# Attention and a gated feed-forward layer on one core: a weight's sign made on GpSimd, the byte of its low word written into it, and all engine orders worked out anew

## The chip, the cores and the metric

The kernel runs on one core of a Trainium2 chip. The metric is the device time of one execution in microseconds (us), as a median of several runs. The engines are called PE (TensorE, the matmuls), DVE (VectorE), ACT (ScalarE), POOL (GpSimd) and SP (SyncE, which here only issues transfers). Each engine works through its own instructions in the order in which they stand; engines wait for each other by semaphores.

## The reference

```python
def attention(q, k, v):                      # 8 batches, 8 heads, 576 positions, 64 wide
    k_p = k.reshape(B, H, 72, 8, D).mean(axis=3)
    v_p = v.reshape(B, H, 72, 8, D).mean(axis=3)
    scores = scale * np.matmul(q, k_p.transpose(0, 1, 3, 2))
    attn = np.exp(scores - np.max(scores, axis=-1, keepdims=True))
    attn = attn / (np.sum(attn, axis=-1, keepdims=True) + 1e-09)
    return np.matmul(attn, v_p)

x = attention(q, k, v)                       # as 4608 tokens x 512
h = x @ w_in                                 # 512 -> 2048
g = h * np.clip(h + 3.0, 0.0, 6.0) / 6.0
out = g @ w_out                              # 2048 -> 512
```

`w_in` and `w_out` come as 64-bit floats, seen as pairs of 32-bit words; everything else is 32-bit.

## The kernel before

The 4608 tokens are worked off in blocks of 512, 256 and then 384 tokens. While the feed-forward products of one block run, the attention of the blocks behind it is worked in between them. The first four blocks (`Block`, products at L965 and L995) take each 32-bit operand as a sum of two parts, `hi` and `lo`, and so need the weights as such pairs. The last eight blocks go in four pairs (`super_block`, products `psx` at L1245 and L1368) by seven products of sums of halves; their operands are split likewise (`part`, L1226 on ACT and L1227 on DVE), and their weights come back from a scratch copy in device memory (tiles `wsFalse` and `wsTrue`, loaded by SP).

The weights are made ready once, in 16 slices `f` of the 2048-wide dimension, in class `Prep`. Slices 0 and 15 go in two parts of 128x512 (a half of `w_in`, a half of `w_out`), the other fourteen in one part of 128x1024 each: 18 parts. Each part's raw words lie in `raw`, and a float of 32 bits is put together in a buffer `u` by six steps:

- `low` (L873, ACT) turns the top byte of the low word into a small integer, written to `u` as a 32-bit integer;
- `sign` (L878, DVE) ors the sign bit of the high word into `u`;
- `scale` (L884, ACT) multiplies the high word, taken as a float, by 2^-111, in place;
- `join` (L889, DVE) ors the scaled high word, shifted left by 3, into `u`;
- `hi` (L913, ACT) rounds `u` to the matmul's format into the weight tile `w`;
- `lo` (L918, DVE) subtracts `hi` from `u`.

There are two buffers `u` for slices 0 to 14, one for the even and one for the odd ones.

At the start, ahead of all this, PE runs 26 matmuls on a unit matrix that nobody reads (`idle`, L461), then the first scores (L596) from `kbd` (L410, pooled keys) and the queries. From a product the chain of a tile of attention goes through DVE (`mx`, L600), ACT (the exponentials, L604), DVE (`sm`, L617 to L621), POOL or DVE (the division, L632 and L638), PE (a transposition, L691 and L693), DVE and ACT (its copies `a` and `arem`, L694 and L695), PE again (L772) and ACT and DVE (`xhi`, `xlo`, L777 and L778) to the operand of the feed-forward products.

Later batches take their keys from tiles `kst` (L388, a transfer on SP), which DVE pools (`ksum`, L402) and ACT places (`kbd`, L410), and their values from tiles `vst` (L421 and L424), which DVE adds up in place (L518) and splits (`vhi` L529 on ACT, `vlo` L530 on DVE). `kst`, `vst` and some others share a ring of four buffers: a load waits until the last reader of the tile that had the buffer is through, and what stands behind it on SP waits too.

The order of each engine's instructions isn't that of the code: `put_in_order` takes a table of numbers for each engine (`ORDER`: PE, DVE, Activation, Pool, SP), which says which instruction of those that the code records stands next.

Of the kernel before, what the change touches and what calls it, by code (L numbers as in the profile page):

```python
# [8 lines left out]
F32 = mybir.dt.float32  # L9
# [249 lines left out]
def attention_moe_kernel(  # L259
# [584 lines left out]
    class Prep:  # L844
# [695 lines left out]
    def run(steps, lag, attention, first_slot=0, preps={}, more=(), hooks={}, share=1.0):  # L1540
# [5 lines left out]
        for u in range(len(steps) + lag):  # L1546
            slot = paced.slot if u >= first_slot else no_slot
            if u < len(steps):
# [4 lines left out]
                if k == NF - 1:  # L1553
                    prep(k, "scale", "low", part=0)
# [115 lines left out]
```

## Time and profile before

| | |
|---|---|
| time, median of 3 runs | 882.92 us (880.13 to 883.78) |
| the profiled execution | 882.52 us, of which the span of its core is 880.6 us |
| mean granted TensorE clock | 0.998 of full speed |
| PE busy | 866.7 us, 98% of the span |
| DVE busy | 677.3 us, 77% |
| ACT busy | 555.9 us, 63% |
| POOL busy | 86.2 us, 10% |

The span runs from the first to the last instruction of the core; the 1.9 us between it and the time of the execution lie around it. A busy share is an average over stages that have different limits.

### The profile page before, as it was taken

How to read it: one execution, taken by the hardware profiler on the slowest of the kernel's cores; microseconds unless marked ns; L12 is line 12 of the kernel's file. 1: busy time of each engine (PE TensorE's matmuls, PEld its weight loads, DVE VectorE, ACT ScalarE, POOL GpSimd, SP SyncE). 2: the span in 40 equal slices, each digit the busy share in tenths (PEclk: the TensorE clock that was granted, in tenths of full speed). 3: DMA queues.
4: the chain of work that ended last, by engine and by line, in shares of the span. 5: the costliest groups of instructions: out<-in, count | busy, mean ns of one | idle time of the engine just before them, and what ended most of it. 6: DMA issues, size and time to landing. Idle time of an engine off the chain costs nothing.

```text
span 880.6 us, 15638 instructions
## 1 busy us (share of the span) xinstructions
PE 866.7 (98%) x5360; PEld 814.2 (92%) x5360; DVE 677.3 (77%) x1340; ACT 555.9 (63%) x1515; POOL 86.2 (10%) x168
## 2 busy tenths in 40 slices
PE   8899999999999999999999999999999999999998
PEld 7788888999999999999888999989999999999998
DVE  5999964677786677887989788897788888466764
ACT  5998666665667564777444777656687756355442
POOL 4100001110211110101000201100111100000000
PEclk9999999999999999999999999999999999999999
DMA  9934314223357998986779978976987777877884
GB/s 323 364 124 157 100 33 138 73 58 111 105 176 254 298 285 265 361 289 194 241 231 289 307 269 286 306 261 203 319 269 242 218 242 245 284 252 242 274 263 135
DMA packets 124654, 200.00 MB, mean 227 GB/s; under 512 B 13216, under 2 KB 81056, under 8 KB 124576
## 3 DMA queue, kind: packets, MB, share of 16 engines
q1 hardware_dynamic: 124432, 199.00, 69.1%
q8 instruction: 43, 0.70, 0.3%
q14 instruction: 35, 0.29, 0.1%
q10 hardware_dynamic: 144, 0.00, 0.0%
HBM read 158.08 MB, written 40.89 MB: 226 GB/s over the span
## 4 chain that ended last, share of the span: by engine, by line
PE 91%; DVE 5%; DMA 2%; ACT 1%; issue 1%; POOL 0%; ACTq 0%; DVEq 0%; POOLq 0%
PE psx L1245 26%; PE psx L1368 17%; PE psh L965 15%; PE pso L995 15%; PE psx L1297 8%; PE psa L596 4%; PE psa L772 4%; PE psa L702 1%; PE idle L461 1%; DMA kst<-k_l 1%; DMA vst<-v_l 1%; DVE part L1227 1%; DVE u L889 0%; DVE g L1325 0%; ACT part L1226 0%
## 5 line engine op out<-in xcount | busy, mean ns | idle before, releaser
L1245 PE MATMUL psx<-x,wsFalse 128*128 128x384 f32 x768 | 151.0, 340 | 0.0
L965 PE MATMUL psh<-xhi,w 128*128 128x384 f32 (+2 forms) x520 | 145.7, 339 | 0.0
L1245 PEld LDWEIGHTS psx<-x,wsFalse 128*128 128x128 f32 x768 | 133.9, 188 | 0.6 <-ACT c L1221 0.2
L1226 ACT CAST part<-g 128x768 fp32r<-128x768 f32 x100 | 83.7, 837 | 67.6 <-PE psx L1368 56.9
L1227 DVE TENSOR_TENSOR part<-g,part 128x768 fp32r<-128x768 f32 x100 | 96.1, 961 | 32.5 <-ACT part L1226 31.2
L995 PE MATMUL pso<-w,ghi 128*128 128x512 f32 x384 | 120.0, 398 | 0.0
L1245 PE MATMUL psx<-x,wsTrue 128*128 128x384 f32 x576 | 114.1, 340 | 0.0
L1368 PE MATMUL psx<-wsFalse,part 128*128 128x256 f32 x864 | 109.7, 284 | 0.0
L1368 PEld LDWEIGHTS psx<-wsFalse,part 128*128 128x128 f32 x864 | 107.1, 191 | 0.2 <-ACT kept L1343 0.2
L1245 PEld LDWEIGHTS psx<-x,wsTrue 128*128 128x128 f32 x576 | 99.8, 188 | 0.4 <-DVE g L1208 0.3
L965 PEld LDWEIGHTS psh<-xhi,w 128*128 128x128 f32 x520 | 93.2, 188 | 6.8 <-ACT xhi L777 0.2
L965 PE MATMUL psh<-xlo,w 128*128 128x384 f32 (+2 forms) x260 | 87.0, 335 | 0.0
L604 ACT ACTIVATE e<-psa,mx 128x72 f32<-128x72 f32 x256 | 78.9, 324 | 12.6 <-DVE mx L600 11.6
L1368 PE MATMUL psx<-wsTrue,part 128*128 128x256 f32 x648 | 82.2, 284 | 2.1 <-ACT part L1226 2.1
L632 POOL TENSOR_TENSOR a<-e,sm 128x256 f32<-128x256 f32 x60 | 44.2, 737 | 407.6 <-DVE sm L621 310.7
L1368 PEld LDWEIGHTS psx<-wsTrue,part 128*128 128x128 f32 x648 | 79.4, 191 | 2.3 <-ACT part L1226 2.3
L995 PEld LDWEIGHTS pso<-w,ghi 128*128 128x128 f32 x384 | 69.2, 188 | 10.4
L1213 DVE TENSOR_TENSOR g<-psx,c 128x384 f32<-128x384 f32 x96 | 52.5, 554 | 26.8 <-PE psx L1245 20.9
L995 PE MATMUL pso<-w,glo 128*128 128x512 f32 x192 | 72.7, 396 | 0.0
L1207 ACT ACTIVATE r<-g,small 128x384 f32<-128x384 f32 x96 | 58.2, 620 | 16.8 <-DVE g L1213 13.7
L1221 ACT COPY c<-psx 128x384 f32<-128x384 f32 x96 | 45.1, 486 | 33.1 <-PE psx L1245 29.2
L1208 DVE SCALAR_TENSOR_TENSOR g<-r,g 128x384 f32<-128x384 f32 x96 | 53.2, 564 | 11.6 <-ACT r L1207 11.1
(134 smaller groups left out, 1474.3 us busy)
## 6 DMA issues: line engine op xcount, KB each, us to landing
wsFalse<-wd SPq DMA_DIRECT2D x64, 512.0 KB, 4.9
wsTrue<-wd SPq DMA_DIRECT2D x48, 512.0 KB, 4.8
wsFalse<-w2d SPq DMA_DIRECT2D x31, 512.0 KB, 5.5
wsFalse<-w2t SPq DMA_DIRECT2D x27, 512.0 KB, 4.8
wsTrue<-w2d SPq DMA_DIRECT2D x21, 512.0 KB, 5.7
wsTrue<-w2t SPq DMA_DIRECT2D x21, 512.0 KB, 4.8
raw<-w_in_l SPq DMA_DIRECT2D x16, 512.0 KB, 8.9
raw<-w_out_l SPq DMA_DIRECT2D x16, 512.0 KB, 8.7
```

The lines of the kernel that those rows point to most:

```text
L604: nc.scalar.activation(self.e[:, h], self.ps[:, h], AF.Exp, bias=self.mx[:, h : h + 1], accum_out=self.sm[:, h : h + 1])
L965: nc.tensor.matmul(self.ps, l[f][:, c, :], r[:, c, :], start=c == 0 and i == 0, stop=c == NCC - 1 and i == 2)
L995: nc.tensor.matmul(pos, l, r, start=f == 0 and i == 0, stop=f == NF - 1 and i == 2)
L1207: nc.scalar.activation(r, src, AF.Relu, bias=half_low, scale=GSCALE / (6.0 * WSCALE))
L1208: nc.vector.scalar_tensor_tensor(out=g_of[i][:, k], in0=r, scalar=GSCALE, in1=src, op0=ALU.min, op1=ALU.mult)
L1213: nc.vector.tensor_tensor(out=g_of[i][:, k], in0=ps, in1=kept, op=ALU.add)
L1221: nc.scalar.copy(c, ps)
L1226: nc.scalar.copy(t[:, 0], src)
L1227: nc.vector.tensor_tensor(out=t[:, 1], in0=src, in1=t[:, 0].bitcast(F32), op=ALU.subtract)
L1245: nc.tensor.matmul(ps, w[:, l, c * P : (c + 1) * P], t[:, r, c], start=o in (1, 2, 5) and c == 0 and k == 0, stop=c == 1 and k == 2, skip_ ...
L1297: nc.tensor.matmul(to, l, w[:, qs, r], start=f == 0 and k == 0, stop=end and k == 2)
L1368: nc.tensor.matmul(to, t[:, l, k, i * P : (i + 1) * P], w[:, k, r], start=begin and k == 0 and y == 0 and i % 2 == 0, stop=m == NM - 1 and ...
```

## The change

`sign` is now the first step of a part and runs on POOL: one instruction multiplies the high word, taken as a float, by 0.0, which gives a zero with that word's sign, and writes it to `u`. `low`, behind it, writes its result as one byte into the lowest byte of each word of `u`, instead of as a 32-bit integer. `scale`, `join`, `hi` and `lo` are as before. 18 instructions leave DVE (14 of 128x1024, 4 of 128x512) and 18 come to POOL. `scale` overwrites the word that `sign` reads, so it now waits for POOL, and `low` waits for it as well.

```diff
+        def sign(self, part):
+            top, _, u = self.words(part)
+            nc.gpsimd.tensor_scalar(
+                out=u, in0=top.bitcast(F32), scalar1=0.0, scalar2=None, op0=ALU.mult
+            )
+
         def low(self, part):
 
             a, b, raw, u = part
             byte = raw.bitcast(U8).rearrange("p i f w -> p (i f) w")[:, :, 3]
-            nc.scalar.activation(u.bitcast(U32), byte, AF.Copy, bias=2.0**-6 - 0.5, scale=2.0**-5)
-
-        def sign(self, part):
-            top, _, u = self.words(part)
-            u = u.bitcast(U32)
-            nc.vector.scalar_tensor_tensor(
-                out=u, in0=top, scalar=0x80000000, in1=u, op0=ALU.bitwise_and, op1=ALU.bitwise_or
-            )
+            to = u.bitcast(U8).rearrange("p (f w) -> p f w", w=4)[:, :, 0]
+            nc.scalar.activation(to, byte, AF.Copy, bias=2.0**-6 - 0.5, scale=2.0**-5)
...
-    prep(0, "scale", "low", part=0)
+    prep(0, "sign", "scale", "low", part=0)
...
-    prep(0, "sign", "join", part=0)
+    prep(0, "join", part=0)
...
                 if k and k + 1 < NF - 1:
-                    prep(k + 1, "scale", "low", "sign")
+                    prep(k + 1, "sign", "scale", "low")
...
     "Pool": """
-        0-1 17 11-12 38 2-3 7-8 10 9 4-6 13-14 16 15 18 37 19-22 24 23 25-28 30 29 55-56 31-36 39-54 57-60 79-80
+        13 1 0 21 2-3 14 8 4 7 11 9-10 5-6 56 19 15 12 16 18 17 22 20 23-32 55 33-40 42 41 43-46 48 47 73-74 49-54
```

All five tables of `ORDER` are replaced, and they move much more than the 18 instructions. PE, ACT and SP still have the instructions that they had. Lines of the changed kernel stand 57 below those of before (L596 is L653), in `Prep` by other amounts: `sign` is L928, `low` L937, `scale` L941, `join` L946, `hi` L970, `lo` L975. Three places show what the tables do.

On PE, at the start: the `idle` matmuls and the first scores (`psa`), before and then changed.

```order
L461 MATMUL idle_174<-ident_76 128x128 x26
L596 MATMUL psa_214<-kbd0_83,stage_133 128x144
L596 MATMUL psa_208<-kbd0_83,stage_133 128x144 x2
L596 MATMUL psa_211<-kbd0_83,stage_133 128x144 x2
L596 MATMUL psa_214<-kbd0_83,stage_133 128x144
```

```order
L518 MATMUL idle_174<-ident_76 128x128 x19
L653 MATMUL psa_208<-kbd0_83,stage_133 128x144
L518 MATMUL idle_174<-ident_76 128x128 x2
L653 MATMUL psa_208<-kbd0_83,stage_133 128x144
L518 MATMUL idle_174<-ident_76 128x128
L653 MATMUL psa_211<-kbd0_83,stage_133 128x144 x2
L653 MATMUL psa_214<-kbd0_83,stage_133 128x144
```

The first score stands behind 19 `idle` matmuls instead of 26; the other seven are spread behind it.

On DVE and POOL, some 20 instructions further: DVE before, with the two `sign` steps (L878) and the two `join` steps (L889) of slice 0 in `u_290`; DVE changed; POOL changed, with the `sign` steps (L928) of slices 0 and 1.

```order
L632 TENSOR_TENSOR stage_133<-stage_133,sm_207 128x256
L638 TENSOR_TENSOR stage_133<-stage_133,sm_207 128x96
L878 SCALAR_TENSOR_TENSOR u_290<-raw_0_145,u_290 128x512
L694 COPY a32_300<-psa_302 128x2x256
L889 SCALAR_TENSOR_TENSOR u_290<-raw_0_145,u_290 128x512
L600 TENSOR_REDUCE mx_326<-psa_334 128x4
L878 SCALAR_TENSOR_TENSOR u_290<-raw_0_148,u_290 128x512
L600 TENSOR_REDUCE mx_328<-psa_347 128x4
L889 SCALAR_TENSOR_TENSOR u_290<-raw_0_148,u_290 128x512
L918 TENSOR_TENSOR w_0_344<-u_290,w_0_344 128x512
L778 TENSOR_TENSOR xlo_341<-psa_337,xhi_340 128x256
L569 TENSOR_TENSOR v1_164<-v1_164 128x4x256
```

```order
L946 SCALAR_TENSOR_TENSOR u_290<-raw_0_148,u_290 128x512
L677 TENSOR_SCALAR sm_205<-sm_205 128x4
L678 RECIPROCAL sm_205<-sm_205 128x4
L678 RECIPROCAL sm_207<-sm_207 128x4
L689 TENSOR_TENSOR stage_133<-stage_133,sm_207 128x256
L751 COPY a32_301<-psa_303 128x2x256
L695 TENSOR_TENSOR stage_133<-stage_133,sm_207 128x96
L657 TENSOR_REDUCE mx_326<-psa_334 128x4
L975 TENSOR_TENSOR w_0_431<-u_290,w_0_431 128x512
L657 TENSOR_REDUCE mx_328<-psa_347 128x4
L946 SCALAR_TENSOR_TENSOR u_290<-raw_0_145,u_290 128x512
```

```order
L549 TENSOR_TENSOR stage_130<-stage_130 32x2x128
L928 TENSOR_SCALAR u_290<-raw_0_148 128x512
L695 TENSOR_TENSOR stage_132<-stage_132,sm_201 128x96
L549 TENSOR_TENSOR stage_130<-stage_130 32x2x64
L689 TENSOR_TENSOR stage_132<-stage_132,sm_201 128x256
L928 TENSOR_SCALAR u_290<-raw_0_145 128x512
L689 TENSOR_TENSOR stage_133<-stage_132,sm_205 128x256
L695 TENSOR_TENSOR stage_133<-stage_132,sm_205 128x96
L551 TENSOR_TENSOR vrem32_176<-stage_130,small_81 32x256 x2
L566 MEMSET vlo_1958 128x512
L928 TENSOR_SCALAR u_450<-raw_1_150 128x1024
L689 TENSOR_TENSOR stage_128<-stage_128,sm_327 128x256
```

The half of `w_out` now comes first, the `v1` additions have gone to places some 40 instructions further on, and on POOL the `sign` steps stand in among the divisions of the first tiles.

On SP, in the second of the four pairs of blocks: `kst_6574`, the first keys of a later batch, before, where it stands last in a row of weight loads; and changed.

```order
L1115 DMA wsFalse_6516<-w2t0_124 128x1024
L421 DMA vst_6524<-v_l 128x2x256
L1115 DMA wsTrue_6554<-w2t1_125 128x1024
L1115 DMA wsTrue_6605<-w2t2_126 128x1024
L1115 DMA wsTrue_6637<-w2t3_127 128x1024
L1115 DMA wsFalse_6662<-w2t0_124 128x1024
L381 DMA qt_6568<-q_l 128x4x128
L1115 DMA wsFalse_6710<-w2t1_125 128x1024
L1115 DMA wsFalse_6755<-w2t2_126 128x1024
L1115 DMA wsTrue_6833<-w2t0_124 128x1024
L424 DMA vst_6570<-vr_l 32x2x256 x3
L1115 DMA wsFalse_6800<-w2t3_127 128x1024
```

```order
L478 DMA vst_6349<-v_l 128x2x256
L478 DMA vst_6524<-v_l 128x2x256
L1172 DMA wsFalse_6395<-w2d1_121 128x2x512
L1172 DMA wsFalse_6430<-w2d2_122 128x2x512
L481 DMA vst_6570<-vr_l 32x2x256
L1172 DMA wsFalse_6465<-w2d3_123 128x2x512
L1172 DMA wsTrue_6554<-w2t1_125 128x1024
L445 DMA kst_6574<-k_l 128x576
L1172 DMA wsFalse_6516<-w2t0_124 128x1024
L438 DMA qt_6568<-q_l 128x4x128
L1172 DMA wsTrue_6605<-w2t2_126 128x1024
L1172 DMA wsFalse_6662<-w2t0_124 128x1024
```

Before, `kst_6574` is the row behind the last one shown; changed, it stands ten rows further ahead, in front of `wsFalse_6516`. In the ring it took the buffer of `vst_6249` before, which `vlo` (L530) reads last; it now takes that of `vst_6524`, which is read last by the addition of `vst_6349` and `vst_6524` on DVE (L575). `ksum_6858`, its reader, stands on DVE 12 places behind that addition; before, 26 places behind the addition of those two tiles:

```order
L575 TENSOR_TENSOR vst_6349<-vst_6349,vst_6524 128x512
L575 TENSOR_TENSOR vst_6249<-vst_6249 128x2x128
L575 TENSOR_TENSOR vst_6249<-vst_6249 128x2x64
L782 TENSOR_TENSOR arem_6532<-psa_6526,arem_6532 32x128
L1382 TENSOR_TENSOR g4_5999<-g4_5999 128x2x384
L1284 TENSOR_TENSOR part_6602<-g4_5999,part_6602 128x768
L657 TENSOR_REDUCE mx_6672<-psa_6674 128x4
L1382 TENSOR_TENSOR g6_6189<-g6_6189 128x2x384
L1284 TENSOR_TENSOR part_6634<-g6_6189,part_6634 128x768
L575 TENSOR_TENSOR vst_6349<-vst_6349 128x2x128
L1284 TENSOR_TENSOR part_6657<-g0_5590,part_6657 128x768
L771 TENSOR_TENSOR alo_6438<-psa_6623,ahi_6437 128x2x128
```

The row behind these is `ksum_6858`: the load and its reader stand in the same run of work, further ahead than before.

In the changed tables PE's work between the blocks is also interleaved matmul by matmul in long stretches, where it stood in groups of three to six.

## Rows read from the trace of the kernel before

**Rows 1.** Busy time by stretch (the span's stretches in us, then for PE, PEld, DVE, ACT and POOL the busy us and the number of instructions; PEclk is the granted clock as a share of 2.4 GHz, then the transfers' share and GB/s).

```profile
10.33:36.31 25.98, 21.06 (x135) 17.60 (x133) 24.35 (x58) 23.22 (x86) 9.24 (x14) 1.00 1.05 385
36.31:117.50 81.19, 81.19 (x388) 67.32 (x387) 76.10 (x116) 68.40 (x133) 0.53 (x1) 1.00 0.39 140
117.50:119.60 2.10, 0.79 (x5) 0.31 (x3) 1.36 (x3) 0.84 (x2) 0.00 (x0) 1.00 0.00 0
119.60:586.00 466.40, 466.40 (x2706) 433.13 (x2707) 359.11 (x809) 296.29 (x914) 57.50 (x111) 1.00 0.69 221
586.00:589.15 3.15, 1.08 (x10) 0.84 (x8) 2.47 (x4) 1.41 (x4) 0.00 (x0) 1.00 0.99 344
589.15:594.00 4.85, 4.85 (x28) 4.85 (x29) 3.93 (x10) 2.80 (x8) 0.00 (x0) 0.65 0.80 302
594.00:877.00 283.00, 283.00 (x2049) 281.99 (x2048) 206.57 (x341) 160.13 (x364) 14.54 (x25) 1.00 0.76 247
```

**Rows 2.** PE in order of time, from three stretches (start, busy us, what, how many; in brackets the idle time before it and what ended it). A matmul on 32-bit operands leaves two records.

```profile
9.44 1.06 PE L461 MATMUL idle<-ident 128*128 128x128 f32 x8
10.33 2.13 PE L596 MATMUL psa<-kbd,stage 128*128 128x144 f32 x16
...
34.66 0.70 PE L772 MATMUL psa<-a,v 128*128 128x256 f32 x2 [1.25 <-DVE a L694]
...
119.53 0.36 PE L772 MATMUL psa<-ahi,vhi 128*128 128x192 f32 x1 [1.31 <-ACT x L774]
...
589.15 0.74 PE L1368 MATMUL psx<-wsTrue,part 128*128 128x256 f32 x4 [2.07 <-ACT part L1226]
```

**Rows 3.** ACT in order of time, from three stretches, with the same columns.

```profile
7.71 0.65 ACT L410 ACTIVATE kbd<-stage 64x144 f32<-64x144 f32 x2 [1.89 <-DVE stage L402]
11.77 0.32 ACT L604 ACTIVATE stage<-psa,mx 128x72 f32<-128x72 f32 x1 [3.40 <-DVE mx L600]
...
20.79 0.62 ACT L913 CAST w<-u 128x512 fp32r<-128x512 f32 x1 [0.77 <-DVE u L889]
...
35.04 1.19 ACT L884 ACTIVATE raw<-raw 128x1024 f32<-128x1024 f32 x1
...
118.64 0.62 ACT L913 CAST w<-u 128x512 fp32r<-128x512 f32 x1 [1.20 <-DVE u L889]
```

**Rows 4.** DVE in order of time, from two stretches, with the same columns.

```profile
18.16 0.94 DVE L878 SCALAR_TENSOR_TENSOR u<-raw,u 128x512 uint32<-128x512 uint32 x1
...
20.99 0.68 DVE L878 SCALAR_TENSOR_TENSOR u<-raw,u 128x512 uint32<-128x512 uint32 x1
...
23.49 1.21 DVE L569 TENSOR_TENSOR v<-v 128x1024 f32<-128x1024 f32 x1
...
25.11 0.66 DVE L569 TENSOR_TENSOR v<-v 128x512 f32<-128x512 f32 x1
...
29.57 1.23 DVE L878 SCALAR_TENSOR_TENSOR u<-raw,u 128x1024 uint32<-128x1024 uint32 x1
...
31.97 0.39 DVE L569 TENSOR_TENSOR v<-v 128x256 f32<-128x256 f32 x1
...
116.44 0.69 DVE L878 SCALAR_TENSOR_TENSOR u<-raw,u 128x512 uint32<-128x512 uint32 x1
```

**Rows 5.** The instructions that write tile `u`, by line (number; shortest, median and longest in ns; first and last start in us; forms).

```profile
L873 ACT ACTIVATE u<-raw x18: 652/1145/1242, 17.3 to 115.7; 128x1024 uint32<-128x1024 uint8 x14, 128x512 uint32<-128x512 uint8 x4
L878 DVE SCALAR_TENSOR_TENSOR u<-raw,u x18: 677/1217/1226, 18.2 to 116.4; 128x1024 uint32<-128x1024 uint32 x14, 128x512 uint32<-128x512 uint32 x4
```

**Rows 6.** Groups of POOL's instructions, shapes apart (busy us, mean ns of one, idle time before and what ended it).

```profile
L509 POOL MEMSET vhi<- 128x512 f32 x7 | 3.7, 527 | 136.6 <-PE psa L772 136.6
...
L380 POOL MEMSET qt<- 128x256 f32 x8 | 2.5, 309 | 34.5 <-DVE vrem L544 32.2 <-DVE vst L518 2.3
```

**Rows 7.** POOL in order of time: one division of attention (L632 with its rest, L638) in each of two stretches.

```profile
180.30 0.61 POOL L632 TENSOR_TENSOR a<-e,sm 128x256 f32<-128x256 f32 x1 [2.57 <-ACT ahi L713]
180.88 0.29 POOL L638 TENSOR_TENSOR ar<-e,sm 128x64 f32<-128x64 f32 x1
...
364.84 0.75 POOL L632 TENSOR_TENSOR a<-e,sm 128x256 f32<-128x256 f32 x1 [1.31 <-DVE sm L621]
365.56 1.00 POOL L638 TENSOR_TENSOR ar<-e,sm 128x64 f32<-128x64 f32 x1
```

**Rows 8.** DVE in the second of these stretches.

```profile
365.04 1.36 DVE L1227 TENSOR_TENSOR part<-g,part 128x768 fp32r<-128x768 f32 x1
...
366.71 0.52 DVE L1208 SCALAR_TENSOR_TENSOR g<-r,psx 128x384 f32<-128x384 f32 x1
```

**Rows 9.** The group of the first of these instructions on the page (busy us and mean ns of one; idle time before).

```profile
L1227 DVE TENSOR_TENSOR part<-g,part 128x768 fp32r<-128x768 f32 x100 | 96.1, 961 | 32.5 <-ACT part L1226 31.2
```

**Rows 10.** The chain that ended last, in order of time, from 560 to 600 us (start, us, what).

```profile
569.83 0.68 DVE vst L518
...
575.67 0.29 DVE vlo L530
...
579.51 7.38 DMA kst<-k_l
586.92 0.77 DVE ksum L402
...
588.26 0.84 ACT part L1226
```

More of the change, by code (lines that the diff above doesn't have):

```diff
@@ new lines @@
+        3090-3092 3027 3093 3108-3109 3028 2999-3001 3132 3094-3098 3133 3099-3101 3110 3144 3102-3103 3145
+        3111-3116 3126-3127 3117-3125 3128-3131 3134-3143 3146-3151 3162-3163 3152-3161 3164-3169 3180-3181 3029
+        3048-3051 3170-3179 3182-3187 3198-3199 3188-3197 3200-3203 3076-3079 3204-3215 3222-3226 3104-3106
+        3216-3221 3107 3227-3257 3348-3349 3258-3259 3270-3271 3356-3357 3260-3269 3272-3277 3288-3289 3350-3355
+        3278-3287 3290-3295 3306-3307 3296-3305 3308-3313 3324-3325 3388-3393 3358-3364 3314-3323 3326-3329
@@ new lines @@
+        3624-3625 3641 3595 3599 3626 3596-3597 3582 3565 3600-3601 3657-3658 3566 3659 3598 3660 3602 3661
+        3603-3604 3665 3611 3627 3642 3612 3635 3666 3662 3628 3613 3643 3614 3636 3667 3644-3648 3629-3634
+        3668-3676 3649-3650 3663-3664 3677-3678 3651-3656 3708-3713 3685-3690 3694-3701 3716-3719 3691-3693
+        3679-3684 3714-3715 3720-3721 3736-3741 3722-3727 3742-3744 3702-3707 3757-3762 3769-3770 3745-3750
+        3730-3735 3870-3872 3728-3729 3751-3756 3763-3768 3771-3782 3789-3793 3783-3788 3794-3829 3840-3841
@@ L252 @@
[L252 to L253 removed]
+        1 0 4 3 2 5-7 11 8-10 12-14 19 18 15 21 16-17 20 31 25-26 32 27 22 51 28 34 29 23 48 30 24 35 33 44 36 43 52
+        45 39 46 41 37 40 38 47 42 49-50 59 53-54 60 55 61 56-58 63-65 62 67-68 66 70-71 69 73 76 80-83 77 92-95
+        74-75 86-88 100-103 78-79 72 89 112-115 106 91 107 109 122-125 110-111 133-136 118 128 144-147 129-131
@@ L254 @@
+        431-432 428 430 434 433 436-439 435 440 443 445 444 446 441 448 447 442 449-450 456 451-455 458 457 459-474
+        477 475 478-482 476 483-492 497 493 495 494 498 500 503 496 499 501-502 504-507 509 508 510-511 513 512
+        514-528 530 529 531-538 541 539 542-546 540 547-555 557 556 558-560
     """,
@@ L1448, in attention_moe_kernel @@
     av(0, *at_A, 1)
-    prep(0, "scale", part=1)
+    prep(0, "sign", "scale", part=1)
     b[1].top()
@@ L1460, in attention_moe_kernel @@
     b[0].divide(nc.gpsimd)
-    prep(0, "sign", part=1)
     a[0].h()
@@ L1483, in attention_moe_kernel @@
     av(0, *at_B, 1)
-    prep(1, "scale", "low")
+    prep(1, "sign", "scale", "low")
     b[3].invert()
@@ L1489, in attention_moe_kernel @@
     transposes_of_half(B, 1, by_dve)
-    prep(1, "sign", "join")
-    prep(2, "scale")
+    prep(1, "join")
+    prep(2, "sign", "scale")
     later = []
@@ L1498, in attention_moe_kernel @@
     prep(1, "lo")
-    prep(2, "low", "sign")
+    prep(2, "low")
     pool_second(*second)
@@ L1553, in run @@
                 if k == NF - 1:
-                    prep(k, "scale", "low", part=0)
+                    prep(k, "sign", "scale", "low", part=0)
                 x.relu()
@@ L1557, in run @@
                 if k == NF - 1:
-                    prep(k, "sign", "join", part=0)
+                    prep(k, "join", part=0)
                 elif k:
@@ L1568, in run @@
                     prep(k, "hi", "lo", part=0)
-                    prep(k, "scale", "low", "sign", "join", part=1)
+                    prep(k, "sign", "scale", "low", "join", part=1)
                 elif preps and u == len(steps) - 2:
```

411 lines of the change are left out of this document (226 added, 185 removed).

## The prediction

> **What bounds the kernel now.** I read the busy time by stretch first, to see where PE, the busiest engine, is not fed. It has work without a gap in every long stretch: 81.19 of 81.19 us, 466.40 of 466.40, 283.00 of 283.00 [rows 1]. PE's work itself is not changed: same matmuls, another order. So DVE's 76.10 busy us of the 81.19 that follow the start are no bound as long as PE finds its operands, and 18 instructions fewer on DVE give nothing there. Time can only go where PE waits: in the start, 10.33 to 36.31 us, where it is busy for 21.06 of 25.98 us and so idle for 4.92; at 118 us, 1.31; at 587 us, 2.07, behind which the granted clock falls to 0.65 of 2.4 GHz over 4.85 us, a mix of its two levels, which costs another 4.85 x 0.35 = 1.7 us [rows 1, 2]. Ahead of 10.33 PE runs `idle` matmuls. I then followed each of these waits back on the engine that ended it, by PE's, ACT's and DVE's order of time and the chain of waits [rows 2, 3, 4, 10].
>
> The sum is made against the profiled execution, 882.5 us, which is 0.4 below the median of 882.9 and well inside the runs' own spread. About 0.5% (4.4 us) is what a measurement of this kernel can tell from no change: faster means below 878.5, slower above 887.3.
>
> **The change, part by part.**
>
> *The start, DVE and ACT.* DVE loses `sign` of slice 0 twice and of slice 1 (0.94, 0.68, 1.23 us), and the additions of `v1` (1.21, 0.66, 0.39) are put off [rows 4]. Together that is 5.1 us of 24.35, on an engine that is nearly full there [rows 1]; but ACT is nearly full too (23.22 of 25.98), and its work does not leave it. On ACT the `scale` of slice 3, 1.19 us at 35.04, is put behind the start, and a wait of 0.77 for `join` should go, since `join` no longer stands behind `sign`; against that, half of the four `kbd` steps, 0.65, moves in from ahead of the first score [rows 3]. Net: 1.19 + 0.77 - 0.65 = 1.3 us less on ACT. DVE's larger relief is then hidden by ACT, so I take **-1.3**.
>
> *The start, the fillers.* Eight records of `idle`, four matmuls, take 0.89 us up to the first score at 10.33: 0.22 each [rows 2]. Seven fewer stand ahead of it, 1.5 us. The keys are placed by 7.71 + 0.65 = 8.36, and ACT then waits 3.40 us for the maxima of these scores [rows 3], so the whole chain moves forward by up to that much: **-1.5**. If the queries' transfer is what is late (the transfers are full in this stretch, 1.05 [rows 1]), the term is nothing.
>
> *The new `sign` on POOL.* No row shows this operation. POOL writes 128x512 in 0.527 us and 128x256 in 0.309 when it only fills [rows 6], which is 0.85 ns a column, so 0.96 us for 128x1024; its product of two operands takes 0.61 us for 256 columns and 0.29 for 64 [rows 7], 1.67 ns a column, so about 1.9 us for 1024. One operand in and one out lies nearer to the fill: I take 1.1 us, 0.55 for a half, and keep 0.96 to 1.9. POOL is busy for 9.24 us of the start and for 0.53 of the next 81 [rows 1], so even 1.9 fits; beyond the start its cover is this idle time, and ACT's `scale` and `low`, which now wait for it, can have it done a slice ahead.
>
> *What it costs DVE.* Where a DVE operation with two operands in SBUF meets a product on POOL, both are longer: the split at 365.04 takes 1.36 us against a mean of 0.961, and POOL's two products beside it 0.75 and 1.00 against 0.61 and 0.29 [rows 7, 8, 9]. One that reads PSUM is at its usual 0.52 [rows 8]. `join`, `lo` and the sums of `v1` are of the first kind. In the start I take one such meeting on the path: 1.36 - 0.96 = **+0.4**.
>
> [...]
>
> *`low` as a byte.* ACT takes 1.145 us at the median for 128x1024 from bytes to words [rows 5]; the same elements to bytes, I take zero. Bounds: 0.1 either way on each, of the size of the spread of this line (1.242 against 1.145), and only those of the start count: ±0.4.
>
> *The wait at 118 us.* On DVE `sign` starts at 116.44 for the last half; ACT's `hi` then sits idle 1.20 us for `join`, and PE's wait of 1.31 ends with an ACT copy that stands behind `hi` [rows 2 to 4]. With `sign` done early on POOL, `join` moves up by its 0.69 and, reordered, need not stand behind other work. I take the whole: **-1.3**; what is next late is the copy's own product, which is ready.
>
> *The wait at 587 us.* The chain runs from the `vst` addition at 569.83 over `vlo` (575.67) to `kst`, which is issued at 579.51, when a ring buffer is free and SP reaches it, and takes 7.38 us; `ksum` and an ACT instruction in its turn then hold PE [rows 10, 2]. In the new tables `kst_6574` takes a buffer that such an addition frees, and stands ahead of weight loads on SP. So it starts some 6 to 10 us earlier. What is queued behind it on SP is `wsFalse_6516`; with the addition earlier too I price that at nothing. Both the wait and the clock behind it go: -2.07 - 1.7 = **-3.8**.
>
> *New waits.* Long stretches of PE's order are made anew, and the old order had two late waits in 800 us. I put in one of the mean size of these two, (1.31 + 3.8) / 2 = **+2.5**; bounds nothing and two of the larger kind, +7.6.
>
> Sum: -1.3 - 1.5 + 0.4 - 1.3 - 3.8 + 2.5 = -5.0; 882.5 - 5.0 = **877.5 us**.
>
> **Rivals.**
>
> 1. *No new wait, and more of the start goes.* All -7.5 without the +2.5 gives 875.0; with the whole idle time of the start (4.92 and the fillers' 1.5 in place of 2.4) 871.0. For it: PE is fed almost everywhere now. Against: ACT is full in the start. About 873, chance 0.14.
>
> 2. [...] Chance 0.20.
>
> 3. *The wait for keys is moved, not removed.* In the new DVE order `ksum_6858` stands 12 places behind the addition that frees its buffer. Between them lie five operations 768 wide at about 0.96 us [rows 9] and six small ones, at most 0.5 each: 4.8 to 7.8 us, against 7.38 for the transfer [rows 10]. DVE can stand there up to 2.6 us, and behind it in its queue are the splits that PE reads. Then the -3.8 is exchanged for as much: 881.3. Chance 0.12. That the change doesn't do what it says (`sign` off DVE) I exclude: the new order shows it.
>
> 4. *Slower: POOL's `sign` blocks DVE in full.* At 1.9 us for 128x1024, with every one of them against a DVE operation of two SBUF operands: in the start slices 0 to 2 hold DVE for 5.7 us where 2.85 are saved, +2.9. In the 81 us behind it 13 more signs' worth at 1.9 against 1.22 [rows 5] adds 8.8 us to an engine with 81.19 - 76.10 = 5.1 to spare [rows 1], +3.7. It decides from 5.1 / 13 + 1.22 = 1.6 us a `sign`. The fillers still give 1.5, and the late gains are taken back by the new waits: 882.5 + 2.9 + 3.7 - 1.5 = 887.6. Against: it needs the upper price and a meeting each time. Chance 0.12.
>
> **How the numbers follow.** The forecast, with its own range of 875 to 879, has 0.42; the rivals 0.14, 0.20, 0.12 and 0.12. Faster: the forecast but for its upper edge, 0.36, and rival 1: 0.50. Slower: 0.12. The same: 0.38. For the range I go from 872.0 (the ceiling of 871.0 needs everything) to 885.5, short of rival 4: some 0.04 lie below and 0.13 above.
>
> **What would show it.** Right: the first score some 1.5 us earlier; PE idle for about 2 us less from there to the last scores of the start; `sign` on POOL at 1.0 to 1.2 us; no PE wait near 118 and none for `kst` near 587, and no stretch at 0.65 behind it. [...]

## The result, and the profile after

The changed kernel takes 887.47 us (median of 6 runs, 886.97 to 888.16), beside 883.6 us of the kernel before on the same chip: 1.0053 times as long, 95% interval 1.0038 to 1.0069. The forecast was 877.5 with a range up to 885.5. The profiled execution of after is at 886.97 us, its span at 885.2. The sign steps did leave DVE (busy time and number of instructions of each engine, before and then changed):

```profile
PE 866.7 (98%) x5360; PEld 814.2 (92%) x5360; DVE 677.3 (77%) x1340; ACT 555.9 (63%) x1515; POOL 86.2 (10%) x168
```

```profile
PE 869.3 (98%) x5360; PEld 810.4 (92%) x5360; DVE 663.3 (75%) x1322; ACT 557.4 (63%) x1515; POOL 132.5 (15%) x186
```

The groups of the instructions that write `u` in the changed kernel, to be held against [rows 5] (number; shortest, median, longest in ns):

```profile
L928 POOL TENSOR_SCALAR u<-raw x18: 1506/2845/3627, 13.2 to 118.3; 128x1024 f32<-128x1024 f32 x14, 128x512 f32<-128x512 f32 x4
L937 ACT ACTIVATE u<-raw x18: 777/1381/1397, 15.3 to 122.1; 128x1024 uint8<-128x1024 uint8 x14, 128x512 uint8<-128x512 uint8 x4
L946 DVE SCALAR_TENSOR_TENSOR u<-raw,u x18: 679/1225/2155, 17.1 to 123.0; 128x1024 uint32<-128x1024 uint32 x14, 128x512 uint32<-128x512 uint32 x4
```

`sign` takes 2.85 us on POOL, not 1.1, and lies above the upper bound of 1.9. `low`'s bytes cost 1.38 us against 1.145. Two of the `join` steps take 2.1 us, against 1.225 at the median.

Busy time by stretch, to be held against [rows 1] (PE's busy us stands first behind the length):

```profile
10.33:36.31 25.98, 21.97 (x142) 18.68 (x142) 22.07 (x54) 23.21 (x87) 18.37 (x21) 1.00 1.06 376
36.31:117.50 81.19, 77.79 (x360) 62.27 (x359) 67.06 (x98) 67.73 (x125) 37.29 (x14) 1.00 0.41 145
117.50:130.00 12.50, 12.50 (x67) 10.63 (x66) 7.17 (x13) 9.18 (x24) 1.53 (x1) 1.00 0.01 3
586.00:600.00 14.00, 13.35 (x112) 13.11 (x111) 13.69 (x24) 7.51 (x16) 0.00 (x0) 1.00 0.92 310
```

PE is idle for 3.4 us between 36 and 117.5, where it never was; the wait at 118 is gone, and so are the one at 587 and the low clock behind it. PE in order of time, the first score and the new waits:

```profile
8.78 0.41 PE L653 MATMUL psa<-kbd,stage 128*128 128x144 f32 x2
...
59.58 0.47 PE L1022 MATMUL psh<-xhi,w 128*128 128x512 f32 x1 [1.56 <-DVE g L1034]
88.35 0.50 PE L1022 MATMUL psh<-xhi,w 128*128 128x512 f32 x1 [0.53 <-ACT w L970]
...
113.51 0.96 PE L1022 MATMUL psh<-xhi,w 128*128 128x512 f32 x3 [0.97 <-ACT w L970]
...
269.15 0.41 PE L1022 MATMUL psh<-xhi,w 128*128 128x384 f32 x1 [0.55 <-ACT wq L1124]
...
381.94 0.45 PE L829 MATMUL psa<-ahi,vhi 128*128 128x384 f32 x1 [0.34 <-DVE alo L771]
...
594.45 0.41 PE L759 MATMUL psa<-ident,a 128*128 128x128 f32 x2 [0.65 <-DVE arem L782]
```

The largest of the early waits, followed back. POOL, then DVE, in order of time:

```profile
55.80 2.83 POOL L928 TENSOR_SCALAR u<-raw 128x1024 f32<-128x1024 f32 x1 [4.85 <-DVE w L975]
```

```profile
54.50 1.21 DVE L975 TENSOR_TENSOR w<-u,w 128x1024 fp32r<-128x1024 f32 x1
55.85 2.12 DVE L946 SCALAR_TENSOR_TENSOR u<-raw,u 128x1024 uint32<-128x1024 uint32 x1
...
58.78 0.66 DVE L1034 SCALAR_TENSOR_TENSOR g<-g,psh 128x512 f32<-128x512 f32 x1
```

The `lo` at 54.50 is the last reader of one `u`: its end lets POOL's next `sign` start, and it lets DVE go on to the `join` of the other `u`. So the two start 0.05 us apart; `join` takes 0.9 us more than its 1.22, and the gate `g` that PE waits for stands behind it.

Eleven of the fourteen `sign` steps of 128x1024 start when a `lo` ends. Beside five of these (at 55.80, 66.53, 89.64, 94.89 and 102.99 us) an instruction with two operands in SBUF, which DVE starts within 0.3 us, takes 0.7 to 0.9 us longer than usual: `join` twice, `glo` (L1042, the low part of the gate's result) twice, `vrem` (L601, a rest of the values) once. Beside the other six none with two operands is longer by more than 0.1 us. One with `glo`, whose usual time is 0.69 (POOL, then DVE):

```profile
66.53 2.84 POOL L928 TENSOR_SCALAR u<-raw 128x1024 f32<-128x1024 f32 x1 [3.02 <-DVE w L975]
```

```profile
66.56 1.62 DVE L1042 TENSOR_TENSOR glo<-g,ghi 128x512 fp32r<-128x512 f32 x1
```

**A ledger of PE.** PE's work is the same in all these kernels, so a time before the n-th feed-forward product (4500 records) splits into work and idle time: I take the start of that record and subtract all work ahead of it, each record at the pitch that records of its shape have in a row (0.120, 0.174 and 0.232 us for 256, 384 and 512 columns of feed-forward products; 0.111 for 128 or 192, 0.122 for 144 and 0.175 for 384 columns of attention). `idle` matmuls count as idle, and so does what a record takes beyond its pitch. The difference of this to the kernel before, in us, gained or lost between five records (with the time at which they start in the kernel before):

| kernel | up to 43 | 43 to 112 | 112 to 125 | 125 to 577 | 577 to 622 | behind | all |
|---|---|---|---|---|---|---|---|
| changed | -0.64 | +5.11 | -1.48 | +4.08 | -2.82 | +0.36 | +4.61 |

Of the 5.1 us from 43 to 112 the rows above show 3.4 as idle time of PE; the rest lies within records, whose ends the profile models. The experiments below go on with this table.

### The profile page after: what moved, and what is told of

The parts are those of the page before. It is cut to its first block, busy times and chain, and to the rows that moved or that the text cites. A ratio compares the mean times of both kernels' runs of the same rounds, so it can differ in the third digit from the quotient of the medians.

```text
span 885.2 us, 15650 instructions
## 1 busy us (share of the span) xinstructions
PE 869.3 (98%) x5360; PEld 810.4 (92%) x5360; DVE 663.3 (75%) x1322; ACT 557.4 (63%) x1515; POOL 132.5 (15%) x186
## 4 chain that ended last, share of the span: by engine, by line
PE 79%; DVE 8%; DMA 6%; ACT 4%; issue 2%; SPq 0%; POOL 0%; ACTq 0%; DVEq 0%; POOLq 0%
PE psx L1302 24%; PE psx L1425 17%; PE pso L1052 11%; PE psh L1022 11%; PE psx L1354 7%; PE psa L653 3%; PE psa L829 3%; DMA raw<-w_out_l 2%; DMA raw<-w_in_l 2%; DVE u L946 2%; DVE part L1284 1%; PE psa L759 1%; ACT w L970 1%; ACT u L937 1%; DVE g L1382 1%
## 5 line engine op out<-in xcount | busy, mean ns | idle before, releaser
L1302 PE MATMUL psx<-x,wsFalse 128*128 128x384 f32 x768 | 164.8, 342 | 0.0
L1022 PE MATMUL psh<-xhi,w 128*128 128x384 f32 (+2 forms) x520 | 149.9, 343 | 3.9 <-ACT w L970 1.8
L1052 PE MATMUL pso<-w,ghi 128*128 128x512 f32 x384 | 130.1, 401 | 0.0
L1302 PE MATMUL psx<-x,wsTrue 128*128 128x384 f32 x576 | 127.0, 344 | 0.2 <-DVE g L1270 0.2
```

The costliest lines, as they stand in the source:

```text
L1022: nc.tensor.matmul(self.ps, l[f][:, c, :], r[:, c, :], start=c == 0 and i == 0, stop=c == NCC - 1 and i == 2)
L1052: nc.tensor.matmul(pos, l, r, start=f == 0 and i == 0, stop=f == NF - 1 and i == 2)
L1302: nc.tensor.matmul(ps, w[:, l, c * P : (c + 1) * P], t[:, r, c], start=o in (1, 2, 5) and c == 0 and k == 0, stop=c == 1 and k == 2, skip_ ...
```

## The experiments

Theory 1: the step itself (POOL, the bytes) makes the waits. Theory 2: the new orders do.

**Step and orders exchanged.** `n_newstep_oldorder` has the new step in the orders of before, `o_oldstep_neworder` the old step in the new orders. First lines of the tables that carry the step, POOL's against the changed kernel's and DVE's against it:

```diff
     "Pool": """
-        13 1 0 21 2-3 14 8 4 7 11 9-10 5-6 56 19 15 12 16 18 17 22 20 23-32 55 33-40 42 41 43-46 48 47 73-74 49-54
+        0-1 21 12-13 56 2-3 7-8 11 10 9 14 4-6
+        19 15-16 20 18 17 22-33 55 34-40 42 41 43-46
     "DVE": """
-        1 0 3-4 2 5 9 6-7 10 8 17 11-12 18 13-14 38 15-16 19-20 22 21 25 45 27 23-24 28 31 80 33 32 34 29 35 26 37
+        1 0 3-4 2 5 9 6-7 10 8 17 11-12 18 13-14 34 40 15-16 19-20 22 21 26 47 28 23-25
```

> The new sign step on POOL (and low as a byte) with the orders of before; only scale is put directly ahead of low on ACT, since it now waits for POOL. Theory 1, the step itself (2.85 us on POOL, 1.38 for low) makes the chain of a slice too long and PE waits for weights between 36 and 118 us: the waits are there with the old orders too, at least 5 us of them, and the wait at 587 us stays: 887 to 892 us. Theory 2, the new orders make the waits and the step is harmless: no waits of PE between 40 and 115 us, 881 to 884.

> The old step on DVE, put directly ahead of join, in the new orders of all engines. Theory 1: the five waits of PE between 57 and 113 us (5.3 us in the changed kernel) are gone or under 1.5 us in sum, the late part is that of the changed kernel (1.6 us worse than before): 882 to 885 us. Theory 2: the waits between 57 and 113 us stay, at least 4 us, and DVE's 17 us more of work add to them: 887 to 890.

Measured: 910.16 us (1.0306, 1.0289 to 1.0323) and 899.18 us (1.0177, 1.0164 to 1.019). Both are far above what either theory expected. From the tables of waits (us in total, times, longest), ACT and PE of the first, then ACT and PE of the second:

```profile
ACT raw L941 <- POOL u L928: 26.4, 11, 4.0
...
PE pso L1052 <- ACT ghi L1038: 5.2, 2, 3.6
PE psa L829 <- ACT x L831: 3.0, 2, 1.5
```

```profile
ACT w L913 <- DVE u L889: 20.2, 13, 2.6
...
PE psh L965 <- ACT w L913: 6.2, 6, 2.2
```

With the new step in the old orders `scale` stands on ACT for 26.4 us waiting for POOL, and the copies and splits that PE needs stand behind it in the queue; in the changed kernel this wait does not occur. With the old step in the new orders ACT waits 20.2 us for `join`, which stands behind `sign` on DVE. As placed here, step and order fit only each other (how much of the loss comes from the places that I gave the moved steps isn't shown), and the question "one or the other" was put wrongly. It is asked again below with the new orders held fixed.

**Early and late orders.** `h1_new_early` takes the changed kernel for all that starts before 124 us in the kernel before and the old orders behind that; `h2_new_late` the reverse, with the old step. The last lines of POOL's table in the first:

```diff
     "Pool": """
-        57-72 75-79 82 80 97 81 84 83 98 85-90 115-116 91-92 94 93 95-96 99-100 102 101 104 103 105-114 117 119 118
+        42 41 43-46 48 47 73-74 49-54 57-72 75-78 97-98 79-90 115-116
+        91-96 99-114 117-120 139-140 121-132 157-158 133-138 141-144 146 145 147-156 159-174
...
```

> The changed kernel for all work that starts before 124 us in the kernel before, the orders of before for the rest. The ledger of PE's idle time says that the changed kernel is 3.0 us behind at that point and loses 1.6 more behind it: by it 886.6 us, with the wait at 587 us back and none at 268, 381 and 520. If instead the late orders only lose because the early part runs late: 885 or less.

> The kernel before, old step and old orders, for all work that starts before 124 us, the new orders for the rest. By the ledger 883.6 + 1.6 = 885.2 us: 3.0 us gained at 587, some 4.6 lost in waits that the new orders make at 268, 381 to 430, 520, 574 and 600 to 700, with no sign step near. If those waits come from running late instead: 880 to 881.

Measured: 886.71 us (1.0036, 1.0022 to 1.0049), as forecast, and 886.28 us (1.0029, 1.0017 to 1.004), 1.1 us above its forecast.

| kernel | up to 43 | 43 to 112 | 112 to 125 | 125 to 577 | 577 to 622 | behind | all |
|---|---|---|---|---|---|---|---|
| h1_new_early | +0.21 | +5.20 | -1.54 | +0.33 | +0.30 | +0.70 | +5.20 |
| h2_new_late | +2.04 | +0.01 | +0.01 | +4.68 | -2.85 | +0.39 | +4.28 |

The two halves come apart: the 5 us up to 112 belong to the early part, and some 4 us from 125 to 577 to the late orders alone, with no `sign` anywhere near and whether the early part ran late or not. (Of the 4.68 of `h2_new_late` 1.03 lie ahead of 133 us, where its two orders meet.) In both kernels the same five places, named by the time in the kernel before, hold 3.2 us of it: 263 to 273 us (0.8), 376 to 385 (0.7), 420 to 430 (0.4), 513 to 522 (0.5) and 565 to 575 (0.8). The +2.04 of `h2_new_late` up to 43 us, with the very order of before, is the clock in that execution:

```profile
34.00:40.00 6.00, 4.98 (x16) 4.04 (x17) 5.13 (x9) 4.46 (x10) 0.00 (x0) 0.72 1.05 393
```

The granted clock was 0.72 of full speed here, behind a wait of 1.25 us at 35 us like that in [rows 2]. In the kernel before it shows two levels behind the wait at 587 us, 1.00 up to 590.25 us and 0.50 from 590.50 to 593.75; 0.72 would be a mix of such levels. From 34 to 40 us it was 1.00 in the profiled execution of before, whose `a` came as late. So the ledgers are read from 43 us on, and ahead of that only where the granted clock was 1.00, as in the kernel before, the changed one and `s0_no_sign` below.

**The step taken apart, in the new orders.** `s0_no_sign` has no `sign` and `low` as a word; `s3_fills` fills `u` three times with zeros, `s1_fill` once; `s1_word` is `s1_fill` with `low` as a word; `s_half` does the sign on half the columns and fills the rest. In all of these signs of weights are missing.

```diff
-            nc.gpsimd.tensor_scalar(
-                out=u, in0=top.bitcast(F32), scalar1=0.0, scalar2=None, op0=ALU.mult
-            )
+            for _ in range(3):
+                nc.gpsimd.memset(u, 0.0)
```

> The changed kernel with its orders, but sign is left out and low writes its word as before, so the signs of the weights are missing. Theory 1, the chain of the step on POOL makes the waits of PE between 57 and 113 us (5.3 us): they shrink to under 1.5 us and the time is 881.5 to 883.5. Theory 2, the new orders make them: at least 4 us of them stay, 886 to 888.

> The changed kernel, but sign is three fills of u with zeros on POOL, so the signs are missing. Three fills of 0.96 us are as long as the step (2.85 us), and read nothing from SBUF. If the length of the chain makes the waits: 886.5 to 888.5, like the changed kernel. If it is the meeting with DVE (join takes 2.1 to 2.3 us beside a sign against 1.22): joins of 1.22 throughout, waits shorter by the 0.9 us of each such join in front of one, 883.5 to 885.5.

> The changed kernel, but sign does only the first half of the columns of a part and a fill with zeros the second, whose signs are missing: 1.42 + 0.53 = 1.95 us on POOL, the upper price of the prediction. If the length on POOL decides, each wait behind a late slice is up to 0.9 us shorter: 884.5 to 886. If the orders decide: 887 to 888.

> The changed kernel, but sign is one fill of u with zeros (0.96 us, nothing is read, so the signs are missing); low still writes bytes. Between no sign at all with low as a word (881.15) and three fills (883.63): if the length on POOL makes their difference, 881.2 to 882; if it is low's 0.24 us for each part on ACT, 883 to 884.

> The changed kernel, but sign is one fill of u (0.96 us, signs missing) and low writes whole words over it, as before. Against the same with bytes (s1_fill: 883.5, low 1.38 us for 128x1024) only low's form differs. If the byte form costs ACT's chain 0.24 us a part and so the 1.5 us of PE's waits that a fill leaves between 40 and 113 us: near the kernel without sign, 881 to 882. If the fill itself costs them, which scale and low wait for: 883 to 884.

| kernel | POOL's step, us | median, us (interval of its ratio to before) | 43 to 112 |
|---|---|---|---|
| changed | 2.85, reads | 887.47 (1.0038 to 1.0069) | +5.11 |
| s3_fills | 2.86, no read | 883.63 (0.9999 to 1.0023) | +2.31 |
| s_half | 1.53 reads, 0.52 fill | 883.48 (1.0 to 1.0022) | +2.70 |
| s1_fill | 0.955, no read | 883.52 (0.9983 to 1.0008) | +1.86 |
| s1_word | 0.954, no read, word | 881.6 (0.997 to 0.9996) | +0.47 |
| s0_no_sign | none, word | 881.15 (0.9957 to 0.9984) | +0.40 |

Read from below, 5.11 us is: 0.40 orders, 0.07 the fill, 1.39 the bytes of `low`, 0.45 the step's length (0.96 against 2.86 us), 2.80 that it reads. The shares hang on the order in which the kernels are read: with the short form of the step below, reading costs 5.29 - 1.86 = 3.4 us and the length nothing. In none of these kernels does ACT wait for POOL's `u`, so it isn't `scale`, held up by a slow reader, that makes the difference. The expectation that the length decides fell with `s3_fills` against `s1_fill`. `s_half` lies below both its forecasts: half the reading costs 2.70 - 2.31 = 0.4 us, far less than half of 2.80. The other four came out on the side of the meeting and of the bytes, or (`s0_no_sign`) 0.35 us below the forecast of theory 1. Beside three fills the same `join` is not lengthened (POOL, then DVE):

```profile
55.64 2.98 POOL L929 MEMSET u<- 128x1024 f32 x3 [5.56 <-DVE w L975]
```

```profile
55.65 1.23 DVE L946 SCALAR_TENSOR_TENSOR u<-raw,u 128x1024 uint32<-128x1024 uint32 x1
```

**What the step's operation costs.** `s_forms` puts other operations in its place in single slices.

> The changed kernel, with another operation of POOL in place of sign in most slices (their signs are then missing or changed): slices 0 to 2, 9, 10 and 15 as they are; 3 and 4 the same product with zero read from u itself, without gaps; 5 and 6 the difference of the high words with themselves (two operands, every second word); 7 and 8 the difference of u with itself (two operands, no gaps); 11 and 12 two products in one instruction; 13 and 14 a fill. It prices the step, it isn't a time to compare. If reading every second word makes sign cost 2.85 us for 1024 columns: 3 and 4 take 1.0 to 1.2, 5 and 6 at least 3, 7 and 8 the 1.7 to 1.9 of the other products. If it is the operation with a number: 3 and 4 take 2.85 as well, 5 to 8 all 1.7 to 1.9.

POOL's groups (busy us, mean ns of one):

```profile
L930 POOL TENSOR_SCALAR u<-raw 128x1024 f32<-128x1024 f32 x4 | 11.7, 2937 | 7.1 <-DVE w L985 4.9 <-DVE sm L678 2.2
...
L932 POOL TENSOR_SCALAR u<-u 128x1024 f32<-128x1024 f32 x2 | 5.6, 2780 | 6.1 <-DVE w L985 6.1
L934 POOL TENSOR_TENSOR u<-raw 128x1024 f32<-128x1024 f32 x2 | 4.6, 2282 | 9.7 <-DVE w L985 6.6 <-DMA raw<-w_out_l 3.2
L936 POOL TENSOR_TENSOR u<-u 128x1024 f32<-128x1024 f32 x2 | 3.8, 1896 | 7.7 <-DVE w L985 7.7
L938 POOL TENSOR_SCALAR u<-raw 128x1024 f32<-128x1024 f32 x2 | 2.2, 1114 | 8.1 <-DVE w L985 8.1
L940 POOL MEMSET u<- 128x1024 f32 x2 | 1.9, 956 | 6.5 <-DVE w L985 6.3
```

It is not the reading of every second word (L932 reads without gaps and takes 2.78). One operation with one number takes 2.8 us; two such operations in one instruction, with the same result, take 1.11 (L938). That was the second branch of the forecast, but for L934, which came out above it.

**The cheap form, and the meetings taken away.** `s2_two_products` is the changed kernel with that form. `s2_apart` adds waits: seven signs stand behind the DVE instruction that was lengthened beside them.

```diff
-                out=u, in0=top.bitcast(F32), scalar1=0.0, scalar2=None, op0=ALU.mult
+                out=u, in0=top.bitcast(F32), scalar1=1.0, scalar2=0.0, op0=ALU.mult, op1=ALU.mult
...
+        pool, dve = [[i for i in traced[a:b] if on(i, e)] for e in (mybir.EngineType.Pool, mybir.EngineType.DVE)]
+        for x, y in [(19, 23), (26, 83), (28, 89), (30, 109), (32, 129), (33, 66), (34, 144)]:
+            sync = mybir.DependencyInfo(mybir.DependencyClass.Sync, mybir.DependencyReason.DATA)
+            tc.add_manual_dep(pool[x], dve[y].name, sync, reason="apart")
```

> The changed kernel, with sign as two products in one instruction (by 1.0 and then by 0.0, the same result), which took 1.11 us for 128x1024 where one product took 2.85. It is the price that the prediction took for the step. If the mis-sized price is what failed: PE's waits from 40 to 113 us at most 1.5 us in sum (5.3 in the changed kernel), 881.5 to 883.5. If the orders are what failed: 886 or more.

> Sign as two products, in the new orders, as in s2_two_products (887.3), but seven of the signs (slices 1, 6, 8, 10, 12, 13, 14) wait until the DVE instruction is through that stood lengthened beside them in the changed kernel. If POOL's read holds DVE for about 0.95 us from its start, and these meetings make the difference between reading and filling: join, glo and vrem there at their usual 1.22, 0.69 and 0.34 us, and 883.5 to 885, like the fills. If the waits come from something else in the step: 887.

Measured: 887.26 us (1.0028 to 1.0056), so the price that the prediction had wrong wasn't what the time hung on; the ledger gives +5.29 from 43 to 112. The meeting is as before (POOL, then DVE):

```profile
57.29 1.11 POOL L928 TENSOR_SCALAR u<-raw 128x1024 f32<-128x1024 f32 x1 [6.59 <-DVE w L975]
```

```profile
57.33 2.15 DVE L946 SCALAR_TENSOR_TENSOR u<-raw,u 128x1024 uint32<-128x1024 uint32 x1
```

`s2_apart`: 885.49 us (1.0017 to 1.0038) and +3.46, half a us above its forecast. The seven meetings account for 1.8 us by both measures. That is short of the 2.8 that reading costs. Taken in tens of products, the ledger shows where the rest is: of the 1.15 us that `s2_apart` is behind `s3_fills`, 0.58 come at the gate at 60 us and 0.48 at 94 us. Both places lie behind new meetings, which the delayed signs make. At the gate `join` is free, but the sign now stands beside small steps of attention, of which one (`sm`, 0.42 in the changed kernel) takes 1.09 in front of it, and PE still waits 1.3 us (POOL and DVE, then DVE beside three fills):

```profile
57.84 1.23 POOL L932 TENSOR_SCALAR u<-raw 128x1024 f32<-128x1024 f32 x1 [7.94 <-DMA raw<-w_out_l]
```

```profile
56.53 1.23 DVE L950 SCALAR_TENSOR_TENSOR u<-raw,u 128x1024 uint32<-128x1024 uint32 x1
...
58.01 1.09 DVE L681 TENSOR_SCALAR sm<-sm 128x4 f32<-128x4 f32 x1
```

```profile
57.13 0.51 DVE L677 TENSOR_SCALAR sm<-sm 128x4 f32<-128x4 f32 x1
```

At 94 us the delayed sign meets a `join`, whose 0.4 us more hold up `hi` and, behind it on ACT, the copy `x` that PE needs (POOL, DVE, PE):

```profile
91.08 1.12 POOL L932 TENSOR_SCALAR u<-raw 128x1024 f32<-128x1024 f32 x1 [5.25 <-DVE glo L1046]
```

```profile
91.66 1.62 DVE L950 SCALAR_TENSOR_TENSOR u<-raw,u 128x1024 uint32<-128x1024 uint32 x1 [0.66 <-ACT u L941]
```

```profile
94.52 0.44 PE L833 MATMUL psa<-a,v 128*128 128x64 f32 x2 [0.39 <-ACT x L835]
```

The meetings taken away and the new ones together come to 1.8 + 1.1 = 2.9 us, about what reading costs.

**Towards a faster kernel.** `s2_best` and `s2_apart_late` take the old orders for what starts behind 124 us, but for 540 to 600 us. `b_fix` is the kernel before with its own step and orders, with that stretch in the new orders and, on ACT, the copy of `x` that PE waits for at 118 us put ahead of the rounding `hi` (here the table of ACT, where only this pair and that stretch change):

```diff
     "Activation": """
...
-        156 166 158 161-162 159 170-171 167 163 172 168 164-165 175-176 173 177 174 169 182 178 183 179-181 186 184
+        156 166 158 161-162 159 170-171 167 163 172 168 164-165 175-176 173 177 174 169 178 182 183 179-181 186 184
```

> Sign as two products, the new orders for the work that starts before 124 us, the orders of before for the rest, but for the stretch from 540 to 600 us, which is in the new orders. By the ledgers of PE's idle time: about 1.0 us ahead of the kernel before at 125 us, 1.7 more at 600: 880 to 881.5. If the late orders of before need the old start: 883 or more.

> The same seven waits in s2_best (884.7): new orders up to 124 us and from 540 to 600, orders of before elsewhere. If meetings and late orders add up: 884.7 less the 2 to 3.5 us that apart gains, 881 to 882.5.

> The kernel before, its step and its orders, with two of the late waits mended: on ACT the copy of x that PE waits for at 118 us stands ahead of the rounding of the last weights, and the work that starts between 540 and 600 us stands in the new orders. By the ledger -1.3 and -2.1 (3.7 gained at 587, 1.6 lost at 574 and 593): 880.2 us. If the new orders' window needs what stands ahead of it, the second part is nothing: 882.3.

Measured: 884.67 us (0.9993 to 1.0018), missed, since the early part is no better than the changed kernel's; 882.14 us (0.9975 to 0.9998), as forecast; 880.54 us (0.9959 to 0.9992), 0.3 above its forecast.

| kernel | up to 43 | 43 to 112 | 112 to 125 | 125 to 577 | 577 to 622 | behind | all |
|---|---|---|---|---|---|---|---|
| s2_apart_late | -0.22 | +3.52 | -1.51 | +0.72 | -2.78 | +0.06 | -0.21 |
| b_fix | -0.03 | +0.01 | -1.58 | +1.00 | -2.76 | +0.10 | -3.26 |

`b_fix` beats both kernels, by 2.8 us against the median of the kernel before, with `sign` on DVE: the two late waits could be had without the change of step. Its ledger is of an execution of 879.22 us at a granted clock of 1.00; over its twelve executions the clock lay between 0.996 and 1.00.

## Why the prediction was wrong

By parts, in us, the sum of -5.0 became +4.6: the start -0.6 for -2.4; the stretch up to 112 us +5.1 for nothing; the wait at 118 -1.5 for -1.3; the orders from 125 to 577 +4.1 for the +2.5 of "New waits"; 587 and its clock -2.8 for -3.8; behind that +0.4. What failed are the second and the fourth.

- **The stretch from 36 to 117 us, which the sum holds at nothing:** this step failed first. The prediction argued that PE is fed there and that DVE's 18 fewer instructions gain nothing. That is borne out: with the new orders and no `sign` at all the stretch is still 0.40 us behind (`s0_no_sign`). But it asked only what the stretch could gain; what the step costs was put in for the start alone. It costs 4.7 of the 5.1 us here: 2.8 since POOL's step reads (5.11 for the changed kernel, 2.31 for three fills, which are as long and read nothing), 1.4 for the bytes on ACT, 0.5 for its length.
- **"New waits, +2.5":** this step failed too. The sum assumed one wait of the mean size of the old two. The late orders cost 4.1, in waits of 0.4 to 0.8 us at five places and smaller ones, where PE had waited once; `h2_new_late` shows that these are the orders' own. What makes each of them wasn't followed.
- **"What it costs DVE", +0.4 for one meeting in the start:** a meeting costs DVE up to 0.9, and there are seven with instructions of two operands in SBUF (0.4 to 0.9 each, the seven that `s2_apart` takes away), six of them behind the start. I looked for chance meetings. Five of the seven aren't: the `lo` that releases POOL also lets DVE go on.
- **`low` as a byte, ±0.4, in the start only:** mis-sized and in the wrong place. It is 0.24 us for each part where the bound was 0.1, and 1.4 us at PE behind the start. The medians differ by 1.9 (883.52 and 881.6), the ratios to the kernel before by 0.0013 or 1.1 us, and the intervals of these overlap.
- **The start:** the first score came 1.55 us earlier, as forecast for the fillers, but the start as a whole gave 0.64 us. Without the step it gives 1.46 (`s0_no_sign`), where the forecast for ACT and the fillers was 2.8: too high by 1.3. The step took 0.8 of it, for the +0.4. A forecast of no gain in the start would have been nearer here.
- **The price of `sign`, 1.1 us within 0.96 to 1.9:** wrong by far (2.85), and without weight for the time, as `s2_two_products` shows.
- **The wait at 118 us:** right in size, 1.48 for 1.3, but not by "`sign` done early on POOL". The last `sign` starts at 118.25, later than the 116.44 of before [rows 4], and its `join` at 122.96, 5 us later than before. The order did it: the copies `x` now stand on ACT ahead of that `hi`, and `b_fix` gains as much with that alone. (POOL, then DVE.)

```profile
118.25 1.53 POOL L928 TENSOR_SCALAR u<-raw 128x512 f32<-128x512 f32 x1 [4.42 <-DMA raw<-w_out_l]
```

```profile
122.96 0.69 DVE L946 SCALAR_TENSOR_TENSOR u<-raw,u 128x512 uint32<-128x512 uint32 x1
```

- **The wait at 587 us and the clock behind it:** right, by the mechanism forecast. The 577 to 622 stretch gives 2.82, which is the 3.8 forecast less the new wait of 0.65 at 594 and small ones. The keys of the later batch are loaded 7.6 us earlier than in [rows 10], and `ksum` doesn't wait for them (rival 3 did not come about):

```profile
571.93 0.34 SPq L445 DMA_DIRECT2D kst<-k_l  x1
```

```profile
578.52 0.74 DVE L459 TENSOR_REDUCE ksum<-kst 128x72 f32<-128x576 f32 x1
```

- **Rival 4** named the right engines, POOL holding DVE (`join` at 2.12 us beside a `sign`, 1.22 without), and its 887.6 us is what was measured, in part by luck. It let the new waits take back the late gains, which is about what came (4.1 against 1.5 and 2.8). That `sign` blocks DVE in full was its assumption, which no row showed; by the ends of DVE's instructions less their usual lengths, the meetings that begin with a `lo` hold DVE until 0.95 to 1.04 us after the start of a `sign` of 2.83 to 2.98 us. And it needed the length of the step to decide, from 1.6 us upward, and the fills and the two products show that length has little to do with it; it had a loss in the start where there was a small gain, and no cost of the bytes. I gave it 0.12, since I asked of it a meeting each time and took that to be unlikely. Seven meetings of eighteen were enough.

What stays open: why the new orders wait at their five late places, and why a meeting costs PE in some places and not in others (the `glo` at 66.56 costs it nothing in the ledger).

## What to carry to other kernels

When a step is moved to another engine, ask what releases it and what else that same event releases: where the event that starts the step also lets the other engine go on, the two meet again and again (here in five of eleven such starts), and a sum that counts one chance meeting is far too low. Ask this of every stretch in which the step runs, those where the busiest engine is fed too: a stretch that can gain nothing can still lose. New orders must be priced stretch by stretch like any other part of a change; a ledger of the busiest engine's idle time at the same piece of work, set against that of the kernel before, shows in one table which stretch gains and which loses. And where a change brings a step and orders together, take them apart by stretch and by parts of the step in the fixed orders; exchanging them as wholes showed here only that, as placed, neither fits the other's counterpart.

## What the runs showed of the hardware that I had not expected

- On POOL one product by a number takes 2.85 us for 128x1024 (2.78 read without gaps), two products in one instruction 1.11, a difference of two operands 1.90 (2.28 over every second word), a fill 0.956.
- In the five meetings that begin with a `lo`, POOL's `sign` holds the DVE instruction with two SBUF operands beside it, but not for the whole of POOL's instruction: the `join` at 55.85 ended at 57.97, which is 1.22 us behind 56.75, 0.95 us after the `sign` of 2.83 us had started. The four other meetings give 0.96 to 1.04 in the same way. Beside the `sign` of 1.11 us it is 57.33 + 2.15 - 1.22 = 58.26, 0.97 us after the start at 57.29. So DVE's instruction goes on 0.95 us or so after the start of POOL's, beside either `sign`. Beside a fill, which reads nothing, `join` isn't lengthened (1.23 us at 55.65).
- `sm`, with one operand of 128x4, is longer beside a `sign` too: 1.09 us in the row at 58.01, where it takes 0.17 at the median of the changed kernel.
- ACT's copy of 128x1024 bytes to every fourth byte takes 1.38 us, to whole words 1.145.
